# w1b in two column parts, parameter rows split over two queues, parameter matmul later, table casts on ScalarE

## The chip, the cores and the metric

The kernel runs on one core of a Trainium2 chip. The metric is the device time of one execution in microseconds (us), the median of several executions.

In the profile, PE is TensorE's matmul stream and PEld its weight loads, DVE is VectorE, ACT is ScalarE, SP is SyncE, which here only issues loads and stores. A "q" behind an engine (SPq, ACTq) marks its sequencer. "L253" is a line of the kernel that was profiled, so the same statement has another number in each kernel. A "bank" is one of the kernel's eight PSUM tiles, into which TensorE writes its products and from which ACT or DVE copies them. The "head" is the time before the first matmul with BT.

## The reference, cut to what matters

```python
g = sigmoid((x * gate_w).sum(-1))                    # x: 2048 x 640, bf16
a = SSM(x): dt = exp(log_dt); Lam_bar = exp(dt * Lam); h = Lam_bar * h + B_bar x; y = 2 Re(C h) + x * Dskip
b = gelu(x @ w1 + b1) @ w2 + b2                      # w1: 640 x 1728, w2: 1728 x 640
out = g * a + (1 - g) * b
```

The complex recurrence is done as a real scan in a rotating frame. For that the kernel needs cos and sin of t * theta for 512 positions and 640 states: the tables TCOS and TSIN.

## The kernel before: the parts that the change touches

x comes in four chunks of 512 rows. The kernel starts with the first MLP product of chunk 0 (ff1), whose operands arrive while it runs. So chunk 0 is turned by TensorE in four pieces of 128 rows ("turn", copied from PSUM by "turned"), and ff1 starts on 128-column strips. The SSM's input product with BT ("ssm") follows at 21.6 us.

```python
load_xn(0, 0, 1);  load_w1a(nc.scalar, 0);  load_xn(0, 1, 2);  load_w1a(nc.scalar, 2)
...                                                   # warm-up of ACT's table
load_xn(0, 2, 3); load_xn(0, 3, 4)
rows(nc.sync, prmA[0:KS, :], A_log_dt)                # parameter rows: 5 x 128
rows(nc.sync, prmA[KS:2 * KS, :], A_Lambda_im)
rows(nc.sync, prmA[2 * KS:3 * KS, :], A_Lambda_re)
for kd in (1, 4, 3):
    load_w1a(nc.sync, kd)                             # columns 0 to 767 of w1
...
for kd in range(KD):                                  # columns 768 to 1727: 5 loads of 240 KB
    nc.sync.dma_start(out=w1b[kd][:, 0:F - cut1], in_=B_w1[kd * P:(kd + 1) * P, cut1:F])
...                                                   # transposed loads of BT, chunk 1, CT; w2 in four
```

```python
strip(0, 0, P, True);  turn_all(1);  strip(2, 0, P, False);  strip(0, P, HT, True)
nc.tensor.matmul(pA[:, HT:HT + 3 * KS], lhsT=prmA[:], rhs=ident[:, 0:3 * KS], ...)   # parameters to columns
nc.vector.tensor_copy(out=colA[:], in_=pA[:, HT:HT + 3 * KS])
nc.scalar.activation(out=dt16[:], in_=ldt_c, func=ACT.Exp)
strip(2, P, HT, False, 0, 3);  turn_all(2)
...  # dt32, dtl, th_c, thp_c: five-column DVE operations, then more strips and turn_all(3)
two_banks = [bank(), bank()]                          # after the strips: the first use of w1b
for kd in range(KD):
    for i in range(2):
        ff1_mm(two_banks[i], 0, FA + i, kd)
```

The tables: Sin on 128 positions, doubled to 256 on DVE, copied to bf16 on DVE (ten casts of 128x256), and turned by a fixed angle for positions 256 to 511.

## Time and profile before

| | before |
|---|---|
| time, median of 3 (lowest to highest) | 216.25 us (215.86 to 216.48) |
| span in the profile | 214.7 us |
| PE busy | 209.7 us, 98% |
| chain of waits: on PE, on a DMA | 93%, 3% |

The page's first part for the kernel before gives, for each engine, its busy time, its share of the span and its instructions.

```profile
PE 209.7 (98%) x1366; PEld 117.1 (55%) x1385; DVE 190.2 (89%) x396; ACT 101.4 (47%) x183; POOL 1.1 (0%) x12
```

The weight loads are 1385 and the matmuls 1366.

The page's fourth part is the chain that ended last. Of the chain in order of time, I show the two pieces at the load (start, length, what).

```profile
PE 93%; DMA 3%; SPq 1%; issue 1%; DVE 0%
```

```profile
8.10 6.94 DMA w1b<-in_B_w_dram
15.04 0.05 issue
```

The table of stretches for the kernel before (each engine's busy time and number of instructions in the stretch) shows TensorE full from 21.64 us on: 36.20 of 36.36 us, and 152.94 of 154.00.

```profile
core 0: us, PE busy (x) PEld busy (x) DVE busy (x) ACT busy (x) POOL busy (x), PEclk, DMA share, GB/s
21.64:58.00 36.36, 36.20 (x189) 16.84 (x189) 35.46 (x89) 22.54 (x40) 0.00 (x0) 1.00 0.85 191
58.00:212.00 154.00, 152.94 (x1035) 88.50 (x1046) 138.30 (x258) 63.63 (x118) 0.00 (x0) 1.00 0.08 27
```

The timeline of PE before, around the first use of w1b (start, length, what, how many merged, and the idle time before with its releaser):

```profile
12.54 0.59 PE L253 MATMUL bank<-xT,w1a 128*128 128x512 bf16 x2
12.97 1.89 PE L253 MATMUL bank<-xT,w1b 128*128 128x512 bf16 x8
15.09 0.82 PE L253 MATMUL bank<-xT,w1b 128*128 128x512 bf16 x3 [0.23 <-DMA w1b<-in_B_w_dram]
```

Eight matmuls from 12.97 at one per 0.216 us put the ninth at 14.70. It starts at 15.09: 0.39 us lost to the fifth load of w1b, which landed at 15.04. The 0.23 printed counts from the modelled end of the eighth, so it is less than the loss; read losses from starts.

The timeline of PE before, around the parameter matmul (L329):

```profile
6.36 0.17 PE L329 MATMUL bank<-ident,prmA 128*128 128x15 bf16 x1
6.38 0.33 PE L253 MATMUL bank<-xT,w1a 128*128 128x128 bf16 x3
6.55 0.54 PE L218 MATMUL bank<-ident,xn 128*128 128x128 bf16 x5
6.93 0.83 PE L253 MATMUL bank<-xT,w1a 128*128 128x128 bf16 x9
```

And the timeline of SP before: what it issued, when.

```profile
2.59 0.37 SPq L125 DMA_DIRECT2D prmA<-in_A_log_dt_dram  x1
3.01 0.26 SPq L125 DMA_DIRECT2D prmA<-in_A_Lambda_im_dram  x1
3.85 0.26 SPq L125 DMA_DIRECT2D prmA<-in_A_Lambda_re_dram  x1
4.16 1.30 SPq L122 DMA_DIRECT2D w1a<-in_B_w_dram  x3
6.29 2.24 SPq L145 DMA_DIRECT2D w1b<-in_B_w_dram  x5
```

SP stands from 3.27 to 3.85. In the list of SP's waits this is one line:

```profile
SPq L125 <- DMA w1a<-in_B_w_dram: 0.6, 1, 0.6
```

The semaphores in the trace show why: the 64 loads and stores share eight completion semaphores in turn, and the third parameter row, the ninth load, has the semaphore of the first. That is the first w1a load. The trace shows the semaphore going up in sixteen steps for it, the last at 3.84 us; the row was issued at 3.85.

### The profile page before, as it was taken

Reading aid. Unit: us, or ns where it says so; the run is one execution under the profiler, and the core shown is the slowest. Engines: PE = TensorE matmul, PEld = TensorE weight load, DVE = VectorE, ACT = ScalarE, POOL = GpSimd, SP = SyncE. Lnnn points to the kernel's source line nnn. Section 1 sums busy time; section 2 is a strip of 40 time slices with the busy share of each in tenths; the row PEclk is TensorE's granted clock in tenths of the full one; section 3 lists DMA queues with packets and bytes.
Section 4 is the critical chain, followed back from the end, with each engine's and each line's share of the span. In section 5 each row is a group of like instructions: output and inputs, shape, how many; then the busy total and the mean of one; then the engine's idle time right before and its main releaser. Section 6 shows DMA issues by size and latency. Waiting matters only on the chain.

```text
span 214.7 us, 3536 instructions
## 1 busy us (share of the span) xinstructions
PE 209.7 (98%) x1366; PEld 117.1 (55%) x1385; DVE 190.2 (89%) x396; ACT 101.4 (47%) x183; POOL 1.1 (0%) x12
## 2 busy tenths in 40 slices
PE   8999999999999999999999999999999999999994
PEld 4745444454455644775445577444454567654774
DVE  2899999999999999899999999999999999983153
ACT  3599556665875696302572310356683423204200
POOL 1000000000000000000000000000000000000000
PEclk9999999999999999999999999999999999999999
DMA  6899999993000000051000005100000000100011
GB/s 201 251 177 232 219 220 374 170 225 92 3 0 0 3 2 0 12 183 64 0 0 3 0 0 186 61 2 0 0 3 14 0 3 31 61 31 3 0 66 61
DMA packets 30419, 15.84 MB, mean 74 GB/s; under 512 B 22978, under 2 KB 30402, under 8 KB 30402
## 3 DMA queue, kind: packets, MB, share of 16 engines
q1 hardware_dynamic: 29970, 15.18, 29.3%
q10 hardware_dynamic: 432, 0.43, 0.6%
q8 instruction: 11, 0.18, 0.3%
q14 instruction: 6, 0.05, 0.1%
HBM read 7.48 MB, written 2.62 MB: 47 GB/s over the span
## 4 chain that ended last, share of the span: by engine, by line
PE 93%; DMA 3%; SPq 1%; issue 1%; DVE 0%
PE bank L594 26%; PE bank L253 23%; PE bank L653 20%; PE bank L536 20%; DMA w1b<-in_B_w_dram 3%; PE bank L215 1%; PE bank L610 1%; PE bank L279 1%; SPq L145 1%; PE bank L218 0%; SPq L125 0%; DVE ot L658 0%; DVE xT L225 0%; PE bank L269 0%
## 5 line engine op out<-in xcount | busy, mean ns | idle before, releaser
L594 PE MATMUL bank<-w_sb,gel 128*128 128x128 bf16 (+1 forms) x408 | 56.9, 297 | 0.7 <-issue 0.5
L594 PEld LDWEIGHTS <-gel 128*128 128x128 bf16 x416 | 32.2, 98 | 25.5
L539 ACT ACTIVATE bu<-bank 128x512 bf16<-128x512 f32 x40 | 23.9, 597 | 39.4 <-PE bank L536 39.3
L258 ACT ACTIVATE gel<-bank,colB 128x512 bf16<-128x512 f32 x52 | 34.1, 694 | 11.9 <-PE bank L253 11.1
L653 PEld LDWEIGHTS <-hs 128*128 128x128 bf16 x330 | 31.6, 98 | 11.5
L490 DVE TENSOR_TENSOR_SCAN g<-r_c,carry,v 128x512 bf16<-128x512 f32 x30 | 37.4, 1272 | 0.0
L602 ACT ACTIVATE gb<-bank,gcol 128x512 f32<-128x512 f32 (+1 forms) x32 | 15.1, 527 | 35.4 <-PE bank L610 19.3
L253 PE MATMUL bank<-xT,w1b 128*128 128x512 bf16 x137 | 31.0, 379 | 0.4 <-DMA w1b<-in_B_w_dram 0.2
L253 PE MATMUL bank<-xT,w1a 128*128 128x512 bf16 (+1 forms) x152 | 27.7, 334 | 0.2
L653 PE MATMUL bank<-CT_re,hs 128*128 128x320 bf16 (+2 forms) x165 | 27.1, 295 | 0.0
L653 PE MATMUL bank<-CT_im,hs 128*128 128x320 bf16 (+2 forms) x165 | 27.1, 295 | 0.0
L658 DVE SCALAR_TENSOR_TENSOR ot<-bank,gcol,gb 128x320 bf16<-128x320 f32 (+2 forms) x33 | 17.6, 535 | 9.2 <-PE bank L653 8.7
L536 PE MATMUL bank<-xT,BT_im 128*128 128x512 bf16 x99 | 24.8, 379 | 0.1
L536 PE MATMUL bank<-xT,BT_re 128*128 128x512 bf16 x97 | 24.4, 379 | 0.2
L253 PEld LDWEIGHTS <-w1b 128*128 128x128 bf16 x140 | 13.6, 98 | 16.9 <-DMA w1b<-in_B_w_dram 0.7
L253 PEld LDWEIGHTS <-w1a 128*128 128x128 bf16 x156 | 13.8, 101 | 12.5
L569 DVE TENSOR_TENSOR bank<-xn,Dbc 128x320 f32<-128x320 bf16 (+2 forms) x33 | 14.5, 483 | 3.5 <-ACT gb L602 3.4
L536 PEld LDWEIGHTS <-BT_im 128*128 128x128 bf16 x100 | 9.8, 98 | 11.8
L471 DVE TENSOR_TENSOR v<-wa,wb 128x512 bf16<-128x512 bf16 x40 | 15.2, 421 | 0.6
L536 PEld LDWEIGHTS <-BT_re 128*128 128x128 bf16 x100 | 9.6, 98 | 11.0
L583 ACT ACTIVATE bank<-b2bc 128x512 f32<-128x512 bf16 (+1 forms) x24 | 11.7, 529 | 6.2 <-DVE ot L658 6.2
L471 DVE TENSOR_TENSOR wa<-TCOS,g 128x1024 bf16<-128x1024 bf16 x20 | 13.7, 687 | 0.1
(100 smaller groups left out, 151.5 us busy)
## 6 DMA issues: line engine op xcount, KB each, us to landing
out_dram<-ot SPq DMA_DIRECT2D x15, 160.0 KB, 1.8
xn<-in_A_x_dram SPq DMA_DIRECT2D x6, 320.0 KB, 3.2
w_sb<-in_B_w_dram SPq DMA_DIRECT2D x3, 480.0 KB, 4.0
w1b<-in_B_w_dram SPq DMA_DIRECT2D x5, 240.0 KB, 6.1
xn<-in_A_x_dram SPq DMA_DIRECT2D x4, 160.0 KB, 3.1
w_sb<-in_B_w_dram SPq DMA_DIRECT2D x1, 640.0 KB
w1a<-in_B_w_dram SPq DMA_DIRECT2D x3, 192.0 KB, 2.9
w1a<-in_B_w_dram ACTq DMA_DIRECT2D x2, 192.0 KB, 3.6
```

The source lines that it names most:

```text
L253: nc.tensor.matmul(p[:, t0:t1], lhsT=w, rhs=xT[c][:, kd, t0:t1], start=(kd == 0) if first is None else first, stop=(kd == last), skip_grou ...
L258: nc.scalar.activation(out=gel[c][:, kf, :], in_=p[:, :], func=ACT.Gelu_apprx_tanh, bias=b1_c[:, kf:kf + 1])
L471: nc.vector.tensor_tensor(out=o, in0=a, in1=b, op=op)
L490: nc.vector.tensor_tensor_scan(s["g"][:, ri, :], r_c[:, ks:ks + 1].to_broadcast([P, CH]), s["v"][:, ri, :], init, ALU.mult, ALU.add)
L536: nc.tensor.matmul(p[:], lhsT=BT[ks >= KSA][:, kd, (ks % KSA if ks < KSA else ks - KSA) * P:][:, 0:P], rhs=xT[c][:, kd, :], start=(kd == 0 ...
L539: nc.scalar.activation(out=bu[:, ri, :], in_=p[:], func=ACT.Identity)
L569: dve_now(ck.pe, 0.45, lambda: nc.vector.tensor_tensor(out=p[:, 0:d1 - d0], in0=xn[c][:, a, d0:d1], in1=Dbc[:, d0:d1], op=ALU.mult))
L583: nc.scalar.activation(out=v, in_=src, func=ACT.Identity)
L594: nc.tensor.matmul(p[:, col:col + d1 - d0], lhsT=gel[c][:, kf, a * P:(a + 1) * P], rhs=w2_sb[:, kf, d0:d1], start=False, stop=False, skip_ ...
L602: nc.scalar.activation(out=gbs[ti][:, d0:d1], in_=p[:, col:col + d1 - d0], func=ACT.Identity, scale=gcol[:, 1, ti:ti + 1])
L653: nc.tensor.matmul(p[:, 0:d1 - d0], lhsT=hs[c][:, j, lo:lo + P], rhs=CT[:, j % KS, d0:d1], start=False, stop=(j == 2 * KS - 1), skip_group ...
L658: nc.vector.scalar_tensor_tensor(out=ot[:, d0:d1], in0=p[:, 0:d1 - d0], scalar=gcol[:, 0, ti:ti + 1], in1=gbs[ti][:, d0:d1], op0=ALU.mult, ...
```

## The change

The intent was to start the tables and the second column range of w1 earlier, and to take work off DVE. Its parts: w1b is held and loaded in two column parts (512 columns first, then 448 as w1c); two parameter rows are issued by ACT; the parameter matmul moves behind the turning of the third piece, with one five-column DVE operation less (three in place of four); of the fourth piece, the last turned copy moves from ACT to DVE and another from DVE to ACT; the ten casts become two wide passes on ACT; w2 and two x chunks come in one load each. The change was also named "Sin tables doubled once"; that is no new step, since the kernel before doubled them once too.

```diff
-    w1b = [const.tile([P, n1b], BF16, name=f"w1b_{kd}") for kd in range(KD)]
+    w1b = [const.tile([P, cut2 - cut1], BF16, name=f"w1b_{kd}") for kd in range(KD)]
+    w1c = [const.tile([P, n1c], BF16, name=f"w1c_{kd}") for kd in range(KD)]
+    rows(nc.scalar, prmA[0:KS, :], A_log_dt)
+    rows(nc.scalar, prmA[KS:2 * KS, :], A_Lambda_im)
-    rows(nc.sync, prmA[0:KS, :], A_log_dt)
-    rows(nc.sync, prmA[KS:2 * KS, :], A_Lambda_im)
     for kd in range(KD):
-        nc.sync.dma_start(out=w1b[kd][:, 0:F - cut1], in_=B_w1[kd * P:(kd + 1) * P, cut1:F])
+        nc.sync.dma_start(out=w1b[kd][:], in_=B_w1[kd * P:(kd + 1) * P, cut1:cut2])
+    for kd in range(KD):
+        nc.sync.dma_start(out=w1c[kd][:, 0:F - cut2], in_=B_w1[kd * P:(kd + 1) * P, cut2:F])
-    for k0, k1 in ((0, 3), (3, 6), (6, 9), (9, KF - 1)):
+    for k0, k1 in ((0, KF - 1),):
         nc.sync.dma_start(out=w2_sb[:, k0:k1, :], ...)
-    for a in (0, H):
-        load_xn(1, a, a + H)
+    load_xn(1)                                        # and load_xn(2) likewise
 ...
     strip(0, P, HT, True)
-    nc.tensor.matmul(pA[:, HT:HT + 3 * KS], lhsT=prmA[:], ...)   # colA, dt16
     strip(2, P, HT, False, 0, 3)
     turn_all(2)
-    nc.vector.tensor_copy(out=dt32[:], in_=dt16[:])              # dtl, th_c, thp_c
     strip(2, P, HT, False, 3, FA)
+    nc.tensor.matmul(pA[:, HT:HT + 3 * KS], lhsT=prmA[:], ...)   # colA, dt16, limp
     strip(0, HT, HT + P, True)
-    turn_all(3)
+    turn_all(3, True)                                 # its last copy comes later, on DVE, behind u
 ...
-        nc.vector.tensor_copy(out=TCOS[:, ks, 0:HB], in_=FC[:, ks, :])
-        nc.vector.tensor_copy(out=TSIN[:, ks, 0:HB], in_=FS[:, ks, :])
 ...
+    nc.scalar.activation(out=TCOS[:, :, 0:HB], in_=FC, func=ACT.Identity)
+    nc.scalar.activation(out=TSIN[:, :, 0:HB], in_=FS, func=ACT.Identity)
-    ck.dve = 27.0
+    ck.dve = 25.5
```

More of the change, by code (lines that the diff above doesn't have):

```diff
@@ L79 @@
     cut1 = FA * P
-    n1b = F - cut1 + 1
+    FB = FA + 4
+    cut2 = FB * P
+    n1c = F - cut2 + 1
     xT = [const.tile([P, KD, CH], BF16, name=f"xT{c}") for c in range(NCH)]
     w1a = [const.tile([P, cut1], BF16, name=f"w1a_{kd}") for kd in range(KD)]
-    w1b = [const.tile([P, n1b], BF16, name=f"w1b_{kd}") for kd in range(KD)]
+    w1b = [const.tile([P, cut2 - cut1], BF16, name=f"w1b_{kd}") for kd in range(KD)]
+    w1c = [const.tile([P, n1c], BF16, name=f"w1c_{kd}") for kd in range(KD)]
     w2_sb = const.tile([P, KF - 1, D], BF16, name="w2_sb")
@@ L130 @@
     load_w1a(nc.scalar, 2)
+    nc.vector.memset(prmA[:], 0.0)
+    nc.vector.memset(prmB[:], 0.0)
+    rows(nc.scalar, prmA[0:KS, :], A_log_dt)
+    rows(nc.scalar, prmA[KS:2 * KS, :], A_Lambda_im)
     warm = const.tile([P, 1], F32, name="warm")
@@ L133 @@
     load_xn(0, 2, 3)
-    nc.vector.memset(prmA[:], 0.0)
-    nc.vector.memset(prmB[:], 0.0)
     load_xn(0, 3, 4)
-    rows(nc.sync, prmA[0:KS, :], A_log_dt)
-    rows(nc.sync, prmA[KS:2 * KS, :], A_Lambda_im)
     rows(nc.sync, prmA[2 * KS:3 * KS, :], A_Lambda_re)
@@ L150 @@
     nc.gpsimd.memset(b1x[:, F_LAST:F_LAST + 1], 0.0)
-    span4 = const.tile([P, 4], F32, name="span4")
-    for i, m in enumerate((1.0, float(CH), float(2 * HC), float(HC))):
-        nc.gpsimd.memset(span4[:, i:i + 1], m)
+    NQ = 4
+    spans = const.tile([P, NQ], F32, name="spans")
+    for i, m in enumerate((1.0, float(CH), float(CH // 2), float(CH // 4))):
+        nc.gpsimd.memset(spans[:, i:i + 1], m)
     nc.sync.dma_start(out=b1x[:, 0:F_LAST], in_=B_b1[F - F_LAST:F].rearrange("(o d) -> o d", o=1).to_broadcast([P, F_LAST]))
@@ L242 @@
     dt16 = col("dt16", BF16)
-    dt32 = col("dt32")
     dtl = col("dtl")
-    th_c = col("th_c")
+    limp = col("limp")
     thp_c = col("thp_c")
@@ L251, in ff1_mm @@
     def ff1_mm(p, c, kf, kd, t0=0, t1=CH, first=None, last=KD - 1):
-        w = w1a[kd][:, kf * P:(kf + 1) * P] if kf < FA else w1b[kd][:, (kf - FA) * P:(kf - FA + 1) * P]
+        w, f0 = (w1a, 0) if kf < FA else (w1b, FA) if kf < FB else (w1c, FB)
+        w = w[kd][:, (kf - f0) * P:(kf - f0 + 1) * P]
         nc.tensor.matmul(p[:, t0:t1], lhsT=w, rhs=xT[c][:, kd, t0:t1],
@@ L279, in last_tile @@
                 nc.tensor.matmul(p[:, a * NL:(a + 1) * NL], lhsT=xT[c][:, kd, a * P:(a + 1) * P],
-                                 rhs=w1b[kd][:, n1b - NL:n1b], start=False, stop=(kd == KD - 1), skip_group_check=True)
+                                 rhs=w1c[kd][:, n1c - NL:n1c], start=False, stop=(kd == KD - 1), skip_group_check=True)
                 pe(76)
@@ L313, in strip, with turn_all @@
             ff1_mm(banks[kf], 0, kf, kd, t0, t1, first, 3)
-    def turn_all(a):
+    def turn_all(a, last=False):
         tB = bank()
@@ L319, in turn_all @@
         turned(nc.vector, tB, 0, a, 0, 1)
-        turned(nc.vector, tB, P, a, 1, 3)
+        turned(nc.scalar if last else nc.vector, tB, P, a, 1, 3)
         for i in range(2):
             turn(pA, i * P, a, 3 + i)
-        turned(nc.scalar, pA, 0, a, 3, 5)
-    strip(0, 0, P, True)
-    turn_all(1)
-    strip(2, 0, P, False)
-    strip(0, P, HT, True)
-    nc.tensor.matmul(pA[:, HT:HT + 3 * KS], lhsT=prmA[:], rhs=ident[:, 0:3 * KS], start=True, stop=True, skip_group_check=True)
-    nc.vector.tensor_copy(out=colA[:], in_=pA[:, HT:HT + 3 * KS])
-    nc.scalar.activation(out=dt16[:], in_=ldt_c, func=ACT.Exp)
-    strip(2, P, HT, False, 0, 3)
-    turn_all(2)
-    nc.vector.tensor_copy(out=dt32[:], in_=dt16[:])
-    nc.vector.tensor_tensor(out=dtl[:], in0=dt32[:], in1=lre_c, op=ALU.mult)
-    nc.vector.tensor_tensor(out=th_c[:], in0=dt32[:], in1=lim_c, op=ALU.mult)
-    nc.vector.tensor_scalar(out=thp_c[:], in0=th_c[:], scalar1=INV_2PI, scalar2=None, op0=ALU.mult)
-    strip(2, P, HT, False, 3, FA)
-    strip(0, HT, HT + P, True)
-    turn_all(3)
-    nc.scalar.activation(out=r_c[:], in_=dtl[:], func=ACT.Exp)
-    strip(2, HT, HT + P, False)
-    strip(0, HT + P, CH, True)
-    strip(2, HT + P, CH, False)
-    strip(1, 0, CH, False)
-    HB = 2 * HC
+        if not last:
+            turned(nc.scalar, pA, 0, a, 3, 5)
+    HB = CH // 2
     def scratch(i):
-        return scr[:, i * KS * HC:(i + 1) * KS * HC].rearrange("p (k i) -> p k i", k=KS)
+        return scr[:, i * KS * P:i * KS * P + KS * HC].rearrange("p (k i) -> p k i", k=KS)
     u, red, ab = scratch(0), scratch(1), scratch(2)
-    m1, m2 = scratch(3), scratch(4)
     FSC = hsp.tile([P, 2 * KS, HB], F32, name="hs")
@@ L357 @@
     FC = FSC[:, KS:2 * KS, :]
-    NQ = 4
     two = col("two", n=NQ * KS)
@@ L365 @@
     kk = work.tile([P, KS, HC], I32, name="bu", bufs=8)
-    def over(c):
-        return c.rearrange("p (k o) -> p k o", o=1).to_broadcast([P, KS, HC])
-    nc.vector.tensor_tensor(out=u, in0=tf[:].rearrange("p (o i) -> p o i", o=1).to_broadcast([P, KS, HC]), in1=over(thp_c[:]), op=ALU.mult)
-    nc.vector.tensor_copy(out=kk[:], in_=u)
-    nc.vector.tensor_tensor(out=red, in0=u, in1=kk[:], op=ALU.subtract)
     sth, cth = sq[:, 0:KS], cq[:, 0:KS]
@@ L375, with over @@
     sH, cH = sq[:, 2 * KS:3 * KS], cq[:, 2 * KS:3 * KS]
-    sQ, cQ = sq[:, 3 * KS:4 * KS], cq[:, 3 * KS:4 * KS]
+    def over(c, n):
+        return c.rearrange("p (k o) -> p k o", o=1).to_broadcast([P, KS, n])
+    strip(0, 0, P, True)
+    turn_all(1)
+    strip(2, 0, P, False)
+    strip(0, P, HT, True)
+    strip(2, P, HT, False, 0, 3)
+    turn_all(2)
+    strip(2, P, HT, False, 3, FA)
+    nc.tensor.matmul(pA[:, HT:HT + 3 * KS], lhsT=prmA[:], rhs=ident[:, 0:3 * KS], start=True, stop=True, skip_group_check=True)
+    nc.vector.tensor_copy(out=colA[:], in_=pA[:, HT:HT + 3 * KS])
+    nc.scalar.activation(out=dt16[:], in_=ldt_c, func=ACT.Exp)
+    nc.vector.tensor_scalar(out=limp[:], in0=lim_c, scalar1=INV_2PI, scalar2=None, op0=ALU.mult)
+    strip(0, HT, HT + P, True)
+    turn_all(3, True)
+    nc.vector.tensor_tensor(out=dtl[:], in0=dt16[:], in1=lre_c, op=ALU.mult)
+    nc.vector.tensor_tensor(out=thp_c[:], in0=dt16[:], in1=limp[:], op=ALU.mult)
+    nc.scalar.activation(out=r_c[:], in_=dtl[:], func=ACT.Exp)
+    nc.vector.tensor_tensor(out=u, in0=tf[:].rearrange("p (o i) -> p o i", o=1).to_broadcast([P, KS, HC]), in1=over(thp_c[:], HC), op=ALU.mult)
+    turned(nc.vector, pA, 0, 3, 3, 5)
+    nc.vector.tensor_copy(out=kk[:], in_=u)
+    nc.vector.tensor_tensor(out=red, in0=u, in1=kk[:], op=ALU.subtract)
+    strip(2, HT, HT + P, False)
+    strip(0, HT + P, CH, True)
+    strip(2, HT + P, CH, False)
+    strip(1, 0, CH, False)
     nc.scalar.activation(out=FS[:, :, 0:HC], in_=red, func=ACT.Sin, scale=TWO_PI_M)
@@ L382 @@
     nc.vector.tensor_tensor(out=two[:].rearrange("p (n k) -> p n k", n=NQ), in0=thp_c[:].rearrange("p (o k) -> p o k", o=1).to_broadcast([P, NQ, KS]),
-                            in1=span4[:].rearrange("p (n o) -> p n o", o=1).to_broadcast([P, NQ, KS]), op=ALU.mult)
+                            in1=spans[:].rearrange("p (n o) -> p n o", o=1).to_broadcast([P, NQ, KS]), op=ALU.mult)
     nc.vector.tensor_copy(out=kq[:], in_=two[:])
@@ L393 @@
             for j in range(KD):
-                nc.vector.tensor_copy(out=w1b[j][:, n1b - 1:n1b], in_=pA[:, j:j + 1])
+                nc.vector.tensor_copy(out=w1c[j][:, n1c - 1:n1c], in_=pA[:, j:j + 1])
         for kd in (4, 3):
@@ L405, with double @@
     ff1(0, FA + 2)
-    lo, hi = slice(0, HC), slice(HC, HB)
-    nc.vector.tensor_tensor(out=m1, in0=FC[:, :, lo], in1=over(cQ), op=ALU.mult)
-    nc.vector.tensor_tensor(out=m2, in0=FS[:, :, lo], in1=over(sQ), op=ALU.mult)
-    nc.vector.tensor_tensor(out=FC[:, :, hi], in0=m1, in1=m2, op=ALU.subtract)
-    nc.vector.tensor_tensor(out=m1, in0=FC[:, :, lo], in1=over(sQ), op=ALU.mult)
-    nc.vector.tensor_tensor(out=m2, in0=FS[:, :, lo], in1=over(cQ), op=ALU.mult)
-    nc.vector.tensor_tensor(out=FS[:, :, hi], in0=m1, in1=m2, op=ALU.add)
+    def double(n, i):
+        lo, hi = slice(0, n), slice(n, 2 * n)
+        s, c = (over(t[:, i * KS:(i + 1) * KS], n) for t in (sq, cq))
+        m1, m2 = (scr[:, (3 + j) * KS * P:(3 + j) * KS * P + KS * n].rearrange("p (k i) -> p k i", k=KS) for j in range(2))
+        nc.vector.tensor_tensor(out=m1, in0=FC[:, :, lo], in1=c, op=ALU.mult)
+        nc.vector.tensor_tensor(out=m2, in0=FS[:, :, lo], in1=s, op=ALU.mult)
+        nc.vector.tensor_tensor(out=FC[:, :, hi], in0=m1, in1=m2, op=ALU.subtract)
+        nc.vector.tensor_tensor(out=m1, in0=FC[:, :, lo], in1=s, op=ALU.mult)
+        nc.vector.tensor_tensor(out=m2, in0=FS[:, :, lo], in1=c, op=ALU.mult)
+        nc.vector.tensor_tensor(out=FS[:, :, hi], in0=m1, in1=m2, op=ALU.add)
+    double(HC, 3)
     nsH = col("nsH")
@@ L682 @@
     fin_a(0)
-    load_xn(2, 0, H)
-    load_xn(2, H, TPC)
+    load_xn(2)
     ssm(2, {KS - 1: lambda: first_banks(1)})
```

## The prediction

> **What bounds the kernel now.** The chain of waits lies 93% on TensorE and only 3% on a DMA (the w1b load). From 21.64 us on (table of stretches: 21.64 to 58 busy 36.20 of 36.36 us, 58 to 212 busy 152.94 of 154.00), TensorE streams 512-column matmuls every 0.216 us with only "issue" gaps. So 190 of the 214.7 us is matmul work that the change leaves alone. TensorE never waits for DVE (89%) or ACT (47%) there (list of waits), so DVE time saved buys nothing. Only the first 21.6 us can move.
>
> **TensorE's losses in the head**, from starts of single matmuls:
> - w1b: two starts 0.61 apart in place of 0.216 (14.48, 15.09), released by the landing at 15.04: 0.39 us.
> - around the prmA matmul, colA and the small DVE ops: 0.10 (at 6.66), 0.16 (7.04), 0.08, 0.10: 0.44 us.
> - an issue gap near 9.0: 0.2, stays.
> Ceiling of the gain: 0.8 us, 0.4%.
>
> **Each part.**
> 1. Parameter rows to ACT's queue: two issues of 0.26 to 0.37 us leave SP, but SP stands until 3.85 us anyway: its ninth load waits for the landing of the first w1a load (SP's waits: 0.6). I expect w1a and w1b issues at today's times. [...]
> 2. w1b in two parts: 640 KB must land before the first ten matmuls, not 1200. At the present 175 GB/s from 8.1 to 15.0 us (estimate) it lands near 12, needed at 13 to 14. The 0.39 us stall goes. w1c is needed near 17, lands near 14 to 15. Five more SP issues (0.43 each) push the BT transposes by up to 2 us; they have about 5 in hand.
> 3. colA moved behind chunk turning: of 0.44 us, 0.1 to 0.2 comes back; the rest are PSUM-copy waits that remain. The turned copy now between u and kk on DVE (0.42) makes the Sin argument 0.15 us later. That carries to the colB/w1c copies, which free the next matmul's bank (12.81 now, 12.97 used): a new wait of 0.1 to 0.3 us. Gelu (14.14, behind Sin and a table load of 1.28) moves 0.15 later too; the third kf tile needs its bank then.
> 4. Casts: DVE loses 10 x 0.29 (about 2 us net), ACT gains two 128x1280 passes of 1.3 us (estimate from 0.74 for 640), at 22.3 to 25. The first bu evictions wait 2 us; PE fills a bank per 1.08, ACT drains in 0.6, 8 banks: no PE stall.
> 5. w2 and xn in single loads: not waited for; zero.
>
> **Sum**: -0.39 -0.15 +0.25 = -0.3 us. Predicted 215.9 us (216.25 now; its runs spread over 0.6), range 215.3 to 216.6. Chances: faster by over 2% 0.01, within 2% 0.98, slower by over 2% 0.01.
>
> **If right, the profile shows:** no DMA wait on w1b; first BT matmul at 21.2 to 21.5 in place of 21.64; w1b issued by SP from 6.3 as now; the first kf tile after the strips waiting for a DVE copy (w1c column); two Identity passes of 1.3 us on ACT after gz; DVE's first TCOS multiply near 25.7 in place of 27.58; the same 190 us after.
>
> **What would make it wrong:** SP reaching w1b earlier (more gain); BT transposes landing after 21.5 (TensorE stalls); ACT's casts keeping banks from ssm; an earlier DVE schedule reordering seeds into a bank wait later; issue gaps moving.

## The result, and the profile after

The changed kernel takes 216.00 us (215.86 to 216.19, 4 runs) against 216.33 (215.86 to 216.48, 4 runs). A ratio here is the mean time of one kernel's runs over that of the other's of the same rounds, so it is not quite the ratio of the medians. It is 0.9989, with a 95% interval of 0.9972 to 1.0006: the same time, and no difference is shown.

The first and the fourth part of the page after:

```profile
PE 210.0 (98%) x1385; PEld 116.4 (54%) x1385; DVE 188.4 (88%) x385; ACT 103.3 (48%) x185; POOL 1.1 (0%) x12
```

```profile
PE 96%; DMA 2%; SPq 0%; ACT 0%; DVE 0%; issue 0%
```

No matmul record is missing here, and the "issue" pieces of the chain are gone with the holes. The stretches after, from the first BT matmul to TensorE's end, show no idle time at all:

```profile
21.10:58.00 36.90, 36.90 (x195) 17.07 (x192) 35.96 (x83) 25.20 (x44) 0.00 (x0) 1.00 0.90 199
58.00:211.40 153.40, 153.40 (x1046) 88.36 (x1044) 136.46 (x257) 63.25 (x117) 0.00 (x0) 1.00 0.08 27
```

The timeline of PE after, around the first use of w1b, has no wait:

```profile
12.60 0.38 PE L258 MATMUL bank<-xT,w1a 128*128 128x512 bf16 x1
12.82 2.97 PE L258 MATMUL bank<-xT,w1b 128*128 128x512 bf16 x13
```

Around the parameter matmul (L361) there is a new wait (0.30 us as printed), for ACT's copy (L232), which reads turned tiles from pA, the bank that this matmul writes:

```profile
6.18 0.44 PE L223 MATMUL bank<-ident,xn 128*128 128x128 bf16 x5
6.46 0.33 PE L258 MATMUL bank<-xT,w1a 128*128 128x128 bf16 x3
7.09 0.17 PE L361 MATMUL bank<-ident,prmA 128*128 128x15 bf16 x1 [0.30 <-ACT xT L232]
7.12 0.49 PE L258 MATMUL bank<-xT,w1a 128*128 128x128 bf16 x6
```

SP after, its timeline and the line of its waits:

```profile
3.80 0.33 SPq L128 DMA_DIRECT2D prmA<-in_A_Lambda_re_dram  x1
4.18 1.54 SPq L125 DMA_DIRECT2D w1a<-in_B_w_dram  x3
6.56 2.24 SPq L148 DMA_DIRECT2D w1b<-in_B_w_dram  x5
```

```profile
SPq L128 <- DMA w1a<-in_B_w_dram: 1.2, 1, 1.2
```

The two rows that left SP's queue turned into 0.6 us more of waiting at the same place. The casts, in ACT's timeline after:

```profile
21.80 1.38 ACT L426 ACTIVATE TCOS<-hs 128x1280 bf16<-128x1280 f32 x1
22.96 1.38 ACT L427 ACTIVATE TSIN<-hs 128x1280 bf16<-128x1280 f32 x1
```

DVE's first use of the finished table moves from 27.58 to 25.61 us.

**One trace is not one number.** The first BT matmul starts at 21.64 before and at 21.10 after, which looks like 0.54 us gained. A second trace of the changed kernel has it at 21.70; its strips end at 9.46 in place of 8.85. The cause is TensorE's clock. The trace records when it was granted in full: at 5.89 us in the trace before, 3.65 in the trace after, 6.33 in the second one after. In the trace before, 128-column matmuls start 0.107 us apart until then and 0.056 after it, and a weight load takes up to 0.15 us until then and 0.098 after it. The instant differs from run to run: the twelve recorded ones lie between 3.65 and 6.52 us, though TensorE's first matmul starts at 0.77 us in all fourteen traces. What sets it, the traces do not show.

So I compare stretches, not instants. All fourteen traces, with starts of matmuls in us ("strips" is the last 128-column strip; "BT to last" runs to TensorE's last matmul start, "rest" from there to the end of the span; instants marked ~ are read from the last slow weight load, where the clock record is missing):

| trace | full clock | strips | first w1b | first BT | w1b to BT | BT to last | rest |
|---|---|---|---|---|---|---|---|
| before | 5.89 | 9.01 | 12.97 | 21.64 | **8.67** | 190.15 | 2.95 |
| before, look b0 | 3.95 | 8.81 | 12.77 | 21.07 | 8.30 | 190.15 | 2.95 |
| before, look b1 | 6.52 | 9.29 | 13.25 | 21.53 | 8.28 | 190.15 | 2.96 |
| after | 3.65 | 8.85 | 12.82 | 21.10 | 8.28 | 190.15 | 2.98 |
| after again, a0 | 6.33 | 9.46 | 13.43 | 21.70 | 8.27 | 190.15 | 2.98 |
| e1 | 5.20 | 8.80 | 12.76 | 21.04 | 8.28 | 190.15 | **3.15** |
| e2 | 4.17 | 8.58 | 12.55 | 21.21 | **8.66** | 190.15 | **3.98** |
| e3 | 5.49 | 9.04 | 13.01 | 21.29 | 8.28 | 190.14 | 2.96 |
| e4 | ~4.7 | 8.72 | 12.69 | 20.97 | 8.28 | 190.14 | 2.97 |
| e5 | 6.21 | 9.26 | 13.23 | 21.72 | **8.49** | 190.15 | 2.98 |
| e6 | 6.21 | 9.30 | 13.26 | 21.54 | 8.28 | 190.15 | **3.10** |
| v1 | 4.71 | 8.85 | 12.81 | 21.09 | 8.28 | 190.15 | **3.15** |
| e8 | ~4.9 | 8.64 | 12.60 | 20.88 | 8.28 | 190.14 | 2.95 |
| e9 | 4.59 | 8.67 | 12.64 | 21.19 | **8.55** | 190.15 | 2.95 |

From the end of the strips to the first w1b matmul it is 3.96 or 3.97 us in every one, so that column is left out. Three things vary: the strips (with the clock, the order of work and the landing of small loads), the stretch from w1b to BT (with w1b's landing), and the rest at the end.

### The profile page after: what moved, and what is told of

Read it like the earlier page. It is cut to its first block, busy times and chain, and to the rows that moved or that the text cites. A ratio compares the mean times of both kernels' runs of the same rounds, so it can differ in the third digit from the quotient of the medians.

```text
span 214.2 us, 3547 instructions
## 1 busy us (share of the span) xinstructions
PE 210.0 (98%) x1385; PEld 116.4 (54%) x1385; DVE 188.4 (88%) x385; ACT 103.3 (48%) x185; POOL 1.1 (0%) x12
## 4 chain that ended last, share of the span: by engine, by line
PE 96%; DMA 2%; SPq 0%; ACT 0%; DVE 0%; issue 0%
PE bank L598 27%; PE bank L258 26%; PE bank L657 20%; PE bank L540 20%; DMA xn<-in_A_x_dram 2%; PE bank L614 1%; PE bank L284 1%; PE bank L223 0%; SPq L122 0%; ACT xT L232 0%; DVE ot L662 0%; PE bank L361 0%; PE bank L274 0%; PE bank L390 0%
## 5 line engine op out<-in xcount | busy, mean ns | idle before, releaser
L598 PE MATMUL bank<-w_sb,gel 128*128 128x512 bf16 (+1 forms) x416 | 57.9, 299 | 0.0
L258 PE MATMUL bank<-xT,w1b 128*128 128x512 bf16 x80 | 17.9, 379 | 0.0
L258 PE MATMUL bank<-xT,w1c 128*128 128x512 bf16 x60 | 13.7, 379 | 0.0
```

The costliest lines, as they stand in the source:

```text
L258: nc.tensor.matmul(p[:, t0:t1], lhsT=w, rhs=xT[c][:, kd, t0:t1], start=(kd == 0) if first is None else first, stop=(kd == last), skip_grou ...
L598: nc.tensor.matmul(p[:, col:col + d1 - d0], lhsT=gel[c][:, kf, a * P:(a + 1) * P], rhs=w2_sb[:, kf, d0:d1], start=False, stop=False, skip_ ...
```

## The experiments

Each was timed in five rounds beside the kernel before, except b0 and b1, which are one execution each. "Ratio" is against the kernel before, with its 95% interval.

### a0: the changed kernel again

No edit.

> The changed kernel again, to see how far one trace of the head repeats. Theory (the gain is the w1b stall, 0.4 us, plus about 0.1 from the reordered parameter chain): first BT matmul near 21.1 us again (21.0 to 21.3), no wait of TensorE on w1b, time 0.2 to 0.5 us under the kernel before. Rival (the 0.5 us between the two traces is luck in DMA landings): first BT matmul anywhere from 21.0 to 21.7, time within 0.1 us of before. The second x piece landed at 4.91 in the first trace against 4.48 before; if the rows on ACT's queue cause that it repeats, if it is luck it goes.

Measured: 216.21 us, ratio 0.9994 (0.9973 to 1.0014). The first BT matmul starts at 21.70, outside what the theory expected, with no wait on w1b. In its numbers the rival held (21.0 to 21.7, time within 0.1 us of before: 216.21 against 216.17), but what moved the instant was mainly the clock (6.33) and not a landing of w1b. The instant does not show a gain or a loss; the stretch of 8.27 repeats. The second x piece lands at 4.68, between the 4.48 and 4.91 seen before, so its lateness in the first trace after was no fixed effect.

### e1: the split alone

```diff
 # the kernel before, with
-    w1b = [const.tile([P, n1b], ...) ...]            # one part, five loads of 240 KB
+    w1b = [const.tile([P, cut2 - cut1], ...) ...]    # two parts, as in the change
+    w1c = [const.tile([P, n1c], ...) ...]
```

> The kernel before with only w1b loaded and held in two parts. Theory: the wait on w1b (0.39 us) goes, first BT matmul at 21.2 to 21.3 in place of 21.64; time 0.3 to 0.4 us under before. Rival (the reordered parameter chain brings the gain): the freed time turns into a wait on the bank that the colB copies free or behind gelu, first BT matmul stays near 21.6 and the time stays.

Measured: 216.27 us, ratio 1.0004 (0.9986 to 1.0023). The wait on w1b is gone. The first BT matmul starts at 21.04, even before the theory's 21.2 to 21.3, but that instant carries the clock; the stretch of 8.28 is what shows that the wait went. The time did not fall, which neither theory explains. Two later findings do: the wait is not there in every execution of the kernel before (b0, b1), and the end of the kernel grew from 2.95 to 3.15 us (e8).

### e2: the change without the split

```diff
 # the changed kernel, with
-    w1b, w1c                                          # two parts
+    w1b                                               # one part, five loads of 240 KB, as before
```

> The changed kernel with w1b whole again, everything else of the change kept. Theory: TensorE waits for the fifth w1b load again, which lands near 15 us; first BT matmul back at 21.5 to 21.7, time equal to before within 0.15 us. Rival (reordering brings the gain): first BT matmul near 21.2, time 0.3 us under before.

Measured: 217.43 us, ratio 1.0051 (1.0032 to 1.0070), the only timed kernel that is clearly apart from before. Neither theory had this time. The wait on w1b is back (8.66). Its list of waits has it:

```profile
PE bank L252 <- DMA w1b<-in_B_w_dram: 0.2, 1, 0.2
```

But that is as much as the trace of the kernel before lost, so it does not make 1.1 us. The table does: TensorE's last matmul starts at 211.36 us, and the rest takes 3.98 in place of 2.95 to 2.98. The timeline of e2 shows the last store issued by ACT at 212.00, and the list of SP's waits what SP, which ends the kernel, then waits for:

```profile
212.00 0.37 ACTq L663 DMA_DIRECT2D out_dram<-ot  x1
```

```profile
SPq L721 <- DMA out_dram<-ot: 2.4, 1, 2.4
```

That store lands 2.24 us after the start of its issue (212.00 to 214.24), against 1.47 before (212.44 to 213.91) and 1.50 after (211.89 to 213.39). In e2's DMA records a packet of 8192 bytes of the "instruction" queue (q14 in the page's third part) runs at 213.05 for 0.38 us, among that store's packets. Such packets are in every trace. Fifteen of the sixteen steps by which the store's semaphore tells of its landing had come by 213.60 and the last came at 214.24, while in every other trace the last store's sixteen steps lie within 0.2 us. That the packet held up this last step fits the times, but it is not shown. Counting SP's instructions up to the last packet of 8192 bytes gives 79 or 80 in all fourteen traces, for example 80 (before), 79 (e1), 80 (e2) and 79 (a0): in these traces it comes at one place in SP's own program, to within one instruction. In e2, which has the fewest loads, that place is at the very end.

### e3: the rows back on SP

```diff
 # the changed kernel, with
-    rows(nc.scalar, prmA[0:KS, :], A_log_dt)
-    rows(nc.scalar, prmA[KS:2 * KS, :], A_Lambda_im)
+    rows(nc.sync, prmA[0:KS, :], A_log_dt)
+    rows(nc.sync, prmA[KS:2 * KS, :], A_Lambda_im)
```

> The changed kernel with its two parameter rows issued by SP again. Theory (SP's ninth load waits for the landing of the first w1a load anyway): SP issues the first w1b load at 6.2 to 6.6 as the changed kernel does, first BT matmul at 21.0 to 21.3, same time as the changed kernel within 0.15 us. Rival (the second issuing queue helps): w1b issues 0.5 us or more later, and TensorE waits for w1a or w1b again. A third possibility: the rows on ACT's queue delayed the second x piece; then it lands near 4.5 here and the early strips start 0.3 us sooner.

Measured: 216.16 us, ratio 0.9995 (0.9973 to 1.0017), beside 0.9994 for the changed kernel. SP issues the first w1b load at 6.28, against 6.56 and 6.50 in the two traces after. The second queue brings nothing; the rival is out. So is the third possibility: the second x piece lands at 4.53 here, and at 4.35 to 4.91 in the six traces with the rows on ACT. Whether it costs 0.2 us of issue time can't be said from these traces, because e2 has the rows on ACT too and issues w1b at 6.34.

### e4: the casts back on DVE

```diff
 # the changed kernel, with
-    nc.scalar.activation(out=TCOS[:, :, 0:HB], in_=FC, func=ACT.Identity)
-    nc.scalar.activation(out=TSIN[:, :, 0:HB], in_=FS, func=ACT.Identity)
-    ck.dve = 25.5
+    ck.dve = 27.0                                     # and the ten tensor_copy of before
```

> The changed kernel with the ten casts back on DVE (and the two wide ACT passes gone). Theory (TensorE never waits for DVE after the head): DVE's first TCOS multiply moves back from 25.6 to 26.2 to about 27.3 to 28, the stretch from the first BT matmul to TensorE's last start stays 190.15 us, and the stretch from the first w1b matmul to the first BT matmul stays 8.28; time as the changed kernel within 0.25 us. Rival (the freed DVE time is worth something): 190.15 grows by up to 1.5 us. Second rival (the wide ACT passes cost TensorE banks): 190.15 shrinks.

Measured: 215.93 us, ratio 0.9983 (0.9960 to 1.0005). DVE's first table multiply moves to 27.37, about 1.8 us later than in the trace after, and the stretch from the first BT matmul to TensorE's last is 190.14: DVE's time is worth nothing here, and the wide ACT passes cost nothing. The theory holds and both rivals are out.

### e5: the two parts loaded in the other order

```diff
 # the changed kernel, with
-    for kd in range(KD): ... w1b[kd]                  # then w1c[kd]
+    for kd in range(KD): ... w1c[kd]                  # then w1b[kd]
```

> The changed kernel with the order of its loads swapped: the last columns (w1c) first, then w1b; same pieces, same sizes, same number of issues. Theory (what counts is how many bytes land before the first ten w1b matmuls): the fifth w1b load lands near 14 to 15 us, TensorE waits on w1b again, first w1b matmul to first BT matmul 8.5 to 9.0 in place of 8.28, time 0.2 to 0.6 us above the changed kernel. Rival (smaller pieces by themselves, or more issues, remove the wait): 8.28 stays and no wait on w1b.

Measured: 216.04 us, ratio 0.9993 (0.9967 to 1.0019). TensorE waits on w1b again, and the stretch from w1b to BT is 8.49, 0.21 more than with w1b first: just under what was expected. So smaller pieces by themselves do not remove the wait, and the rival is out. Its list of waits has three waits on w1b:

```profile
PEld L258 <- DMA w1b<-in_B_w_dram: 1.0, 3, 0.5
```

But the theory's reason, the bytes ahead of the use, is not shown. TensorE lost its 0.20 us at the fifth w1b matmul, to the third load. Fifteen of the sixteen steps of that load's semaphore had come by 12.00, well before the first w1b matmul (13.23); the last came at 14.25. The fourth and the fifth load were held up in the same way (13.15 and 14.62, 13.48 and 14.99). An instruction packet of 16384 bytes ran for 0.96 us from 12.11 on, in the midst of these loads. So TensorE waited for one late step, as in e9 below, and the swap may have done no more than put w1b where that delay falls. The profiled execution had a late full clock (6.21), and the time of all runs does not show the difference: expected 0.2 to 0.6 us more, not found.

### e6: e2 with w2 in four loads

```diff
 # e2, with
-    for k0, k1 in ((0, KF - 1),):
+    for k0, k1 in ((0, 3), (3, 6), (6, 9), (9, KF - 1)):
```

> The changed kernel with w1b whole (217.43 us, 1.1 above the others) and the w2 load in four pieces again, which adds three issues to SP long before the end. In that slow run an instruction-queue packet of 8192 bytes (0.38 us) fell at 213.05, among the last store's packets; in all four traces counted it falls when SP has issued its 79th or 80th instruction. Theory: with three more SP instructions it falls some 8 us earlier, the time from TensorE's last start to the end goes from 3.98 back to about 3.0, and the kernel takes 216.2 to 216.7, 0.8 to 1.2 us less than with w2 in one piece; first w1b to first BT matmul stays at 8.6 to 8.7. Rival (whole w1b with the reordered chain costs 1.1 us by itself): time stays near 217.4.

Measured: 216.62 us, ratio 1.0016 (0.9993 to 1.0038), where e2 had 1.0051. The instruction packet falls at 208.55 instead of 213.05, and the rest takes 3.10 in place of 3.98. So e2's 1.1 us lay at its end, and the rival (the whole w1b costs 1.1 us) is out. Of the 0.88 us by which the rest shrank, 0.74 are the last store's landing (1.50 us after its issue in place of 2.24) and 0.14 are two closing waits fewer after it (see e8). e6 changed the place of the instruction packet and the number of loads together, so that the packet caused the late landing is likely but not isolated. The last clause failed: w1b to BT is 8.28. In this execution the whole w1b landed at 12.62 and there was no wait.

### v1: the split, with the parameter matmul in the turn's bank

```diff
 # e1, with the parameter matmul behind turn_all(2)'s first three turns
-    nc.tensor.matmul(pA[:, HT:HT + 3 * KS], lhsT=prmA[:], ...)
+    nc.tensor.matmul(tB[:, 3 * P:3 * P + 3 * KS], lhsT=prmA[:], ...)   # in turn_all(2)
```

> A candidate: the kernel before, w1b in two parts, and the parameter matmul written into the free columns of the bank that holds the third chunk's turned tiles, behind those turns, so that no turn waits for the colA copy. Theory: the gaps of TensorE of 0.10, 0.16 and 0.09 us around the third and fourth chunk fall to 0.1 together, so the end of the strips comes about 0.25 us sooner than in the kernel before at the same instant of full clock (9.01 for 5.89; 8.80 for 5.20), first w1b to first BT matmul 8.28 with no wait on w1b, time 0.3 to 0.6 us under before. Rival (the head ends on the colB copies or gelu, not on the strips): the stretch from the end of the strips to the first w1b matmul grows beyond 3.97 by what the strips gain, and the time stays.

Measured: 216.36 us, ratio 1.0007 (0.9983 to 1.0032). The strips end at 8.85 with full clock at 4.71, no sooner than e1's order (8.80 for 5.20). Gaps of 0.09, 0.10 and 0.16 us remain around the third and fourth piece, and a new one of 0.40 us appears at 7.77, in front of the strips that need the fourth piece. The waits moved; they did not go. The rival didn't hold either: the way from the strips to w1b stayed 3.96. A miss.

### e8: the split, and as many loads as before

```diff
 # e1, with
-    for k0, k1 in ((0, 3), (3, 6), (6, 9), (9, KF - 1)):
+    for k0, k1 in ((0, KF - 1),):                     # w2 in one load
-    for a in (0, H):
-        load_xn(1, a, a + H)
+    load_xn(1)                                        # and load_xn(2)
```

> The kernel before with w1b in two parts (five more loads) and, as the change has them, w2, the second and the third chunk of x in one load each (five fewer): 64 loads and stores again, where the split alone had 69. No other part of the change. Theory (the end of the kernel depends on how many loads and stores there are, through the place of the last store's semaphore among SP's closing waits): from TensorE's last start to the end 2.95 to 3.0 us in place of 3.15; first w1b to first BT matmul 8.28; time 0.1 to 0.3 us under the split alone, that is 0.1 to 0.4 under before, a little better than the changed kernel because its strips keep the order of before. Rival (the end varies by chance): 3.15 stays or any value comes.

Measured: 215.85 us (215.82 to 216.00), ratio 0.9982 (0.9963 to 1.0001). The rest is 2.95 us, w1b to BT is 8.28. Over all traces the rest follows the number of loads and stores: 64 give 2.95 to 2.98 (ten traces), 62 give 3.10, 69 give 3.15 (twice). In the traces before and after, the eight semaphores are used in turn, and SP's five closing waits take them in the same order. With 64 transfers the last store's semaphore is the last one waited for (at 213.93, behind its landing at 213.91, in the trace before; 213.41 and 213.39 after). With 69, three more waits of 0.07 us come after it, in e1 at 213.40, 213.46 and 213.52. In e2, with 59, the last store is waited for first, and four waits follow: 0.28 of its 1.0 us.

This is the fastest median of all, and better than the changed kernel's, by as little as the interval says: it is not shown to be faster than either.

### b0 and b1: the kernel before, two more looks

No edit.

> The kernel before once more, for its trace. Three traces with w1b whole so far: where the instruction packet of 16384 bytes ran at 12.5 and 12.77, before the last w1b packets, the load landed at 15.04 and 14.6 and TensorE lost 0.39 and 0.36 us; where it ran at 13.14 (full clock only from 6.21) the load had landed at 12.62 and nothing was lost. Theory (the wait on w1b is there in some executions only, by the order of that packet and the load's last packets): w1b lands either near 12.6 with the packet after it, and first w1b to first BT matmul is 8.28, or near 14.5 to 15 with the packet before, and it is 8.5 to 8.7. Rival (the wait is always there): 8.67 whatever the packet does.

> As the look before it, a further execution: w1b lands near 12.6 with the packet after it (8.28), or at 14.5 to 15 with the packet before it (8.5 to 8.7); if the theory of chance holds the three traces of this kernel need not agree; the stretch from the first BT matmul to TensorE's last start is 190.15 again.

Measured: 216.08 and 216.41 us, one execution each, state unknown. The stretch from w1b to BT is 8.30 and 8.28: the wait was next to nothing in b0 and absent in b1. The rule failed: w1b landed late in both (14.46 and 14.86), as the instruction packet ran at 12.53 and 12.99, and still nothing was lost. What decides is a race. TensorE needs the fifth load for its ninth w1b matmul, which is due 8 x 0.2157 = 1.73 us after the first:

| trace, w1b whole | ninth due | landed | lost |
|---|---|---|---|
| before | 14.70 | 15.04 | 0.39 |
| b0 | 14.50 | 14.46 | 0.02 |
| b1 | 14.98 | 14.86 | 0 |
| e2 | 14.28 | 14.60 | 0.36 |
| e6 | 14.99 | 12.62 | 0 |

Both sides of the race vary. Where the clock comes late, TensorE comes late too, and the load is there (b1, e6). The wait hides part of the clock's spread, and taking it away gives less than its size in one trace: in the three traces of the kernel before it is 0.39, 0.02 and 0, on average 0.14 us, of three traces only.

Nor was it the bytes that were late. The packets of the whole w1b can be told apart by their size, 640 of 1920 bytes. The last of them had ended by 12.53 in b0, 12.90 in b1 and 12.96 in e2, and 633 of the 640 by 12.7 in the trace before. The landing, which is the last step of the semaphore, came at 14.46 to 15.04.

### e9: ordinary packets behind w1b

```diff
 # the kernel before, with the first piece of w2 ahead of the transposed loads
+    nc.sync.dma_start(out=w2_sb[:, 0:3, :], in_=B_w2[0:3 * P, :]...)
     for r0, r1, part in ((0, KSA * P, 0), (KSA * P, KS * P, 1)):
         nc.sync.dma_start_transpose(out=BT_re[part][:], ...)
```

> The kernel before, w1b whole, with the first 480 KB piece of w2 loaded ahead of the BT transposes in place of behind them; the same number of loads. In four of the five traces with w1b whole its fifth load landed at 14.46 to 15.04, in a burst of semaphore steps right after a group of 256-byte transpose packets that had taken up to 2.9 us each and all ended together, with the instruction packet of 16384 bytes in their midst; in the fifth that packet came later and the load landed at 12.62. Theory (the transposes queued behind w1b, held up together, keep back its completion): with ordinary packets behind it w1b lands at 11.8 to 12.9 wherever the instruction packet falls, no wait on it, first w1b to first BT matmul 8.28; the BT transposes land some 2.5 us later and TensorE still does not wait for them (190.15); time up to 0.3 us under before. Rival (the bytes of w1b, or the instruction packet by itself, make it late): it lands at 14 to 15 again, and where TensorE comes before 12.8 to its first w1b matmul it waits.

Measured: 216.30 us, ratio 1.0009 (0.9984 to 1.0033). The theory fell: the transposes start only at 13.36, and w1b lands at 14.59 all the same; TensorE loses 0.25 us. Its list of waits shows it:

```profile
PEld L254 <- DMA w1b<-in_B_w_dram: 0.9, 2, 0.5
```

The semaphore's sixteen steps tell more. Fifteen had come by 13.32; the last came at 14.59. So one step was late by 1.3 us. An instruction packet of 16384 bytes took 0.95 us from 11.74 on, and the load's last packets run singly, 0.08 us apart, up to 14.05. That the instruction packet held up that one step is my guess from these times; it is not shown. In each of the other five traces with w1b whole, nine or more steps came in one burst, about 13 ns apart (in the trace before fourteen of the sixteen from 14.85 to 15.04, in b0 twelve from 14.32 to 14.46), just as a group of transpose packets of 0.4 to 2.9 us ended; what holds those steps back stays open.

## Why the prediction was right or wrong, point by point

The time (215.9 predicted, 216.00 measured, range 215.3 to 216.6) and the class were right. The main reading was right too: TensorE bounds the kernel, 190.15 us from the first BT matmul on do not change, DVE's time is worth nothing, and only the first 22 us could move. The sum -0.39 - 0.15 + 0.25, however, came out right by luck: its terms were wrong in both directions.

- **w1b in two parts, -0.39.** The split does take the wait away: every kernel with the first part loaded first has 8.27 or 8.28 from w1b to BT (after, a0, e1, e3, e4, v1, e8). The size was that of one trace. The wait is in one of three traces of the kernel before at 0.39, in the others at 0.02 and 0: about 0.14 us on average. The reason, 640 KB in place of 1200 KB at 175 GB/s, is not what the traces show. The packets of the whole w1b were nearly all through by 12.5 to 13 (b0, b1, e2, before); TensorE waited for steps of the semaphore that came 1.6 to 2.3 us after that, and the 175 GB/s count this standstill as transfer. The split helps because the first part is complete, steps and all, by 11.6 us at the latest. The estimate that it would land near 12 came out (11.50 and 11.54). The BT transposes were issued 2.65 us later (11.70 against 9.05, where up to 2 was forecast), and TensorE did not wait for them.
- **The parameter matmul moved, -0.15.** One trace could not tell, for the sign turns with the clock. The matmul now waits 0.46 to 0.47 us for ACT's read of its bank in every trace with the new order. I add up what TensorE loses against one start per 0.056 us, from just before the parameter matmul to the last strip. In the new order that is 0.65 us in all seven traces. In the old order it is 0.46 where the full clock came at 5.20 or later (before, b1, e1), so there the change costs 0.19. But it is 0.52, 0.68 and 0.83 where the clock came at ~4.9, 4.59 and 3.95 (e8, e9, b0): TensorE then reaches the parameter matmul earlier, and in b0 and e9 it waits 0.37 and 0.22 us for the third parameter row to land. The chain of b0 shows this:

```profile
3.88 2.21 DMA prmA<-in_A_Lambda_re_dram
6.14 0.18 PE bank L329
```

So with an early clock the new order saves up to 0.18. It was not isolated in an experiment of its own.
- **A new wait behind the colB copies, +0.25.** It did not come. Counted from the last strip, to take the clock out, the first Sin starts 1.89 us later in both traces of the changed kernel and 1.82 in the one before, so it moved by 0.07 and not by 0.15; the column copies end at 12.71 for a first w1b matmul at 12.82. Strips to w1b stayed 3.96 or 3.97 everywhere.
- **Rows on ACT's queue, 0.** Right, for the reason given: SP's wait grew from 0.6 to 1.2 us, and e3 shows the same time. The two issues that left SP took 0.37 and 0.26 us before; SP waited that time away. The w1b issues were expected at today's 6.3; they came at 6.56 and 6.50.
- **Casts on ACT, 0.** Right: 1.38 us each where 1.3 was estimated, DVE's first table multiply at 25.61 where 25.7 was predicted, no bank wait, and e4 shows no difference.
- **w2 and x in single loads, "zero".** Right only in sum. They take away the five loads that the split adds. Without them the kernel ends 0.2 us later (e1 against e8); with them and without the split it ends 1.0 us later (e2). I had not looked at the end of the kernel at all.
- **The "issue gap near 9.0: 0.2, stays".** It never existed. The first 512-column matmul's record is missing there, one of 19: weight loads start at 9.06 and 9.28, a matmul only at 9.28.
- **First BT matmul at 21.2 to 21.5.** 21.10 and 21.70 in the two traces: no test at all, since the clock's instant moves it by more than the change does.

With the measured terms, about -0.14 from w1b and between -0.18 and +0.19 from the order, by the clock's instant, the expected difference is a few tenths of a microsecond at most, too little to be seen in these runs; that agrees with 0.9989 and 0.9994, where no difference is shown.

## What to carry to other kernels

In a kernel that keeps one engine full, split the trace at points that every version shares and compare the stretches; instants, and a wait read from a single trace, carry the chance of that execution (here the clock's start and the landing of one load). A wait for a landing is a race, so price it over several traces before counting on it; and compare the load's packets with its semaphore's steps before calling the wait a lack of bandwidth, since here nearly all packets were through about 2 us before the landing (633 of 640 by 12.7 us for a landing at 15.04 in the trace before). When a change adds or removes transfers, look at the last microseconds too: the number of transfers decided where the last store stood in the closing waits and where the instruction packet fell (213.05 in e2, 208.55 in e6), and with them the end took up to 1.0 us longer (e2: 3.98 against 2.95 to 2.98), more than any part of the intended change moved.
